# A two-layer spectral and gated-MLP mixer: one written-out order of named operations for a layer, and tables and weights loaded in halves

## The chip, the core and the metric

The kernel runs on one core of a Trainium2 chip. The core has a matrix engine (TensorE, PE in the profile; its weight loads are PEld), a vector engine (VectorE, DVE), a scalar engine (ScalarE, ACT), a general engine (GpSimd, POOL) and a queue engine for transfers (SyncE, SP). Each works through its own list of instructions in order, and semaphores make one wait for another. The metric is the device time of one execution in microseconds; lower is better. Before the change it is 402.71 us, the median of three runs.

## What is computed

The state `x` has 2048 rows of 512 values in bfloat16. Two layers follow each other, and each consists of block A and block B, with the same weights in both layers:

```
x = x + A(layernorm(x))
x = x + B(layernorm(x))

A(x):  X = rfft2(x) over rows and columns
       return irfft2(X * (w_r + i w_i))

B(x):  h  = gelu(layernorm(x) @ w1)                  # 512 x 512
       hs = four column groups of h, shifted by +1, -1, +2, -2 rows
       x1 = x + hs @ w2                              # 512 x 512
       h2 = gelu(layernorm(x1) @ w3) @ w4            # 512 x 1792, 1792 x 512
       return x1 + h2
```

## The kernel before, in words

The state lies in SBUF as `x_state`, 128 partitions by 16 slabs q by 512 columns; row 16 p + q of the input is partition p of slab q. The Fourier transform of block A is written as matrix products against small tables: over p (128 points), over the columns d, and over q (16 points), and back in the reverse order.

The stages, with the lines that the profile shows:

- `first_front` computes the statistics of the first layernorm for all 16 slabs, partly on DVE (`bn_stats`, L201) and partly on ACT (two passes with a running sum, L299 and L212), scales a table by the reciprocal deviation (`Tq`, L252), and does the transform over p (`over_p`, L263 and L265) into V. While ACT works through its passes, its queue also issues the loads of the tables TL (two halves) and TR.
- `middle` goes over 16 frequency blocks b, in units of one or two. `over_d` (L356) makes four matmuls of 256 columns for each b; ACT copies the result to TV. `over_q` (L369 to L371) makes two of 256 and one of 512; ACT copies to X. `weigh` multiplies X by the two planes of W on DVE (Pab, L382), then adds and subtracts the products into Z (L384, L385). `back_q` (L391, L392) makes four matmuls of 256 for each b, and the result is copied to M by ACT or, for the odd b up to 11 and half of b = 15, by DVE (L404). PSUM banks 0 and 1 belong to `over_d`, 2 and 3 to `over_q`, 4 to 7 to `back_q`. The order of these steps is written out in a string `ORDER`, with a name such as `d4` for `over_d` of the unit that begins at 4; each name stands for the matmuls and for the copies and products that follow them.
- `mlp` follows when all of M is there. `back_d` (L450) and `back_p` (L461) finish the inverse transform, a pair of slabs at a time, with ACT copying Y between them; DVE adds the result to the state (L467, L470), even slabs get `bn_stats` on DVE and odd ones a square on ACT. POOL computes from them the two reciprocal deviations that the nested layernorms need (`rstd_twice`, L236 to L242). Then, for four groups of four slabs: normalisation to `xn` (L245), transposes on PE (L493) copied by ACT to xT, `w1` (L508) with a gelu on ACT (L511) into hT, `w2` (L523) on the shifted hT with an add on DVE (L525), a square on ACT, normalisation to x1n, transposes again, and `w3` (L556), 14 blocks of 128 columns for each group with a gelu for each two blocks (L559) into gT, and `w4` (L565) with the add to the state on DVE (L567). The order of these steps is the order of the calls at the end of `mlp`. There all of the inverse transform comes first, `w1` and `w2` alternate with transposes, and the first blocks of `w3` stand among the last `w2`.
- At the end of the first layer, between the last `w4` steps, the next layernorm's statistics, the tables Tq and the transform over p of the second layer are computed; at the end of the second the result is stored.

In `mlp` all PSUM tiles are taken from one ring of eight banks (`banks`).

The schedule is manual: each engine executes its instructions in the order in which the Python code emits them. Loads are issued by SP (`x_state` in eight parts, then W, then G, Tinv, w1 to w4) and by ACT (T, FA, TL, TR). W is loaded plane by plane, w_r ahead of w_i, each with eight loads of 16 or 15 frequency blocks (L167 and L168, alternating) and one for the mirrored rows of b = 0 (L169).

## Time and profile before

| | |
|---|---|
| median of three runs | 402.71 us (402.16 to 403.85) |
| the profiled execution | 403.39 us |
| its span, first to last instruction | 401.4 us |
| PE busy (matmuls) | 359.1 us, 89% of the span |
| ACT busy | 218.8 us, 55% |
| DVE busy | 187.5 us, 47% |
| POOL busy | 63.0 us, 16% |
| mean granted clock of PE | 0.99 |
| moved by DMA | 15.16 MB |

A line of a group of instructions reads: line of the source, engine, operation, output <- inputs by their names in the program, shape, count | busy us, mean ns of one | idle time of the engine just before them, and what ended it. A line of the timeline begins with its start in us from the span's start and its duration; in square brackets stands the time that the engine sat idle before it, and what ended the wait. A line of the chain of work that ended last is start, duration and what ran. A line of the stretches reads: from and to, length, then for each engine the time busy and the number of instructions, then the clock granted to PE (1.00 is full), the share of the transfer engines that was busy, and GB/s. A line of a wait reads: who waited for whom, us in total, number of waits, the longest. Matmuls overlap in their pipeline, so the duration of one is longer than the distance from its start to the next one's.

### The profile page before, as it was taken

To read this page: it belongs to the slowest core of one execution; us is meant where nothing else is said; L and a number is where in the kernel's file an instruction comes from. 1 tells how busy PE (TensorE), PEld (TensorE's weight loads), DVE (VectorE), ACT (ScalarE), POOL (GpSimd) and SP (SyncE) were. 2 spreads that over 40 slices of the span, in tenths; PEclk is the share of its full clock that TensorE was granted. 3 is DMA by queue.
4 is the path that set the end of the run, shared out by engine and by line. 5 is a ranking of instruction groups with operands and counts; after the bars stand their busy time and mean duration, and the time that the engine had idled before them with its cause. 6 is when DMAs were issued, how large, how long until landed. Compare 5 with 4: busy or idle time off the path is not lost.

```text
span 401.4 us, 5501 instructions
## 1 busy us (share of the span) xinstructions
PE 359.1 (89%) x2109; PEld 199.5 (50%) x2144; DVE 187.5 (47%) x461; ACT 218.8 (55%) x327; POOL 63.0 (16%) x162
## 2 busy tenths in 40 slices
PE   0858978889999999999997887789999999999996
PEld 0635656645555444444555655665454544444442
DVE  4817849845346140411745786985445502020122
ACT  4756856887887405043034885788778731505200
POOL 3600004462130000010111000446213000000000
PEclk9998989999999999999999999999999999999999
DMA  8989300000000000000000000000000001010011
GB/s 268 343 184 355 121 0 0 2 2 0 2 1 2 0 0 2 0 0 2 0 2 1 0 2 0 2 1 2 1 2 0 2 13 41 0 39 15 15 51 41
DMA packets 12266, 15.16 MB, mean 38 GB/s; under 512 B 849, under 2 KB 10065, under 8 KB 12113
## 3 DMA queue, kind: packets, MB, share of 16 engines
q1 hardware_dynamic: 11520, 11.34, 9.2%
q10 hardware_dynamic: 720, 3.47, 2.5%
q8 instruction: 17, 0.28, 0.3%
q14 instruction: 9, 0.07, 0.0%
HBM read 12.71 MB, written 2.10 MB: 37 GB/s over the span
## 4 chain that ended last, share of the span: by engine, by line
PE 71%; DVE 10%; ACT 8%; DMA 6%; issue 3%; SPq 1%; ACTq 0%; DVEq 0%
PE ps L565 24%; PE ps L556 24%; PE ps L523 6%; PE ps L508 6%; DVE Pab L382 3%; PE ps L493 3%; DMA W<-in_A_w_r_dram 3%; PE ps L356 2%; ACT TV L142 2%; ACT xT L142 2%; DMA x_state<-in_A_x_dram 2%; PE ps L450 2%; ACT X L142 2%; DVE ln_st L201 1%; ACT Y L142 1%
## 5 line engine op out<-in xcount | busy, mean ns | idle before, releaser
L559 ACT ACTIVATE gT<-ps 128x1024 bf16<-128x1024 f32 x56 | 57.4, 1025 | 80.3 <-PE ps L556 54.4
L556 PE MATMUL ps<-xT,w 128*128 128x512 bf16 x436 | 98.5, 379 | 0.6
L565 PE MATMUL ps<-w,gT 128*128 128x512 bf16 x437 | 97.4, 379 | 0.6
L567 DVE TENSOR_TENSOR x_state<-ps,x_state 128x512 bf16<-128x512 f32 x32 | 22.1, 691 | 127.1 <-PE ps L565 104.3
L565 PEld LDWEIGHTS <-gT 128*128 128x128 bf16 x448 | 43.9, 98 | 52.4
L556 PEld LDWEIGHTS <-w 128*128 128x128 bf16 x448 | 43.6, 98 | 52.0
L525 DVE SCALAR_TENSOR_TENSOR xn<-xn,ln_c,ps 128x512 bf16<-128x512 bf16 x32 | 23.9, 748 | 27.3 <-PE ps L523 22.7
L508 PE MATMUL ps<-xT,w 128*128 128x512 bf16 x126 | 29.5, 379 | 3.9 <-ACT xT L142 3.8
L201 DVE BATCH_NORM_STATS2 ln_st<-x_state 128x6 f32<-128x512 bf16 x43 | 29.4, 683 | 5.8 <-DMA x_state<-in_A_x_dram 5.0
L142 ACT ACTIVATE xT<-ps 128x1024 bf16<-128x1024 bf16 x32 | 31.8, 1021 | 0.0
L382 DVE TENSOR_TENSOR Pab<-X,W 128x1024 bf16<-128x1024 bf16 (+1 forms) x40 | 21.6, 581 | 18.7 <-ACT X L142 10.0
L523 PE MATMUL ps<-w,hT 128*128 128x512 bf16 x124 | 29.9, 379 | 0.3
L217 POOL TENSOR_SCALAR ln_mv<-ln_s 128x4 f32<-128x4 f32 (+2 forms) x21 | 5.8, 275 | 145.9 <-ACT junk L212 145.4
L142 ACT ACTIVATE V<-ps 128x1024 bf16<-128x1024 f32 (+1 forms) x13 | 12.3, 972 | 28.7 <-PE ps L265 28.7
L263 PE MATMUL ps<-Tq,x_state 128*128 128x256 bf16 x64 | 16.3, 295 | 12.4 <-DVE Tq L252 12.3
L142 ACT ACTIVATE TV<-ps 128x1024 bf16<-128x1024 f32 (+1 forms) x20 | 21.5, 1087 | 9.5 <-PE ps L356 9.5
L212 ACT ACTIVATE junk<-xn 128x512 bf16<-128x512 bf16 x32 | 20.1, 630 | 10.0 <-DVE xn L525 8.5
L391 PE MATMUL ps<-TR,Z 128*128 128x256 bf16 x64 | 16.3, 279 | 9.0 <-DVE Z L384 9.0
L356 PE MATMUL ps<-FA,V 128*128 128x256 bf16 x128 | 17.8, 282 | 4.2 <-ACT TV L142 2.1
L508 PEld LDWEIGHTS <-w 128*128 128x128 bf16 x128 | 12.3, 98 | 17.2 <-issue 4.4
L461 PE MATMUL ps<-Y,Tinv 128*128 128x256 bf16 x128 | 16.3, 273 | 4.2 <-ACT Y L142 4.1
L226 POOL TENSOR_TENSOR ln_r<-ln_ve,mhalf 128x4 f32<-128x4 f32 (+1 forms) x19 | 17.8, 937 | 13.9 <-DVE ln_ve L225 12.7
(65 smaller groups left out, 433.4 us busy)
## 6 DMA issues: line engine op xcount, KB each, us to landing
w<-in_B_w_dram SPq DMA_DIRECT2D x2, 1792.0 KB, 12.6
x_state<-in_A_x_dram SPq DMA_DIRECT2D x8, 256.0 KB, 5.4
out_dram<-x_state SPq DMA_DIRECT2D x16, 128.0 KB, 1.8
TL<-tab_TL ACTq DMA_DIRECT2D x2, 768.0 KB, 7.6
TR<-tab_TR ACTq DMA_DIRECT2D x1, 1536.0 KB, 9.9
w<-in_B_w_dram SPq DMA_DIRECT2D x2, 512.0 KB, 4.9
W<-in_A_w_r_dram SPq DMA_DIRECT2D x4, 128.0 KB, 10.2
W<-in_A_w_i_dram SPq DMA_DIRECT2D x4, 128.0 KB, 4.5
```

What stands on the lines that cost most here:

```text
L142: K.nc.scalar.activation(dst, src, ACT.Copy, bias=0.0, scale=1.0)
L201: v.bn_stats(st[:], src)
L212: K.nc.scalar.activation(junk[:], src, ACT.Square, bias=0.0, scale=1.0, accum_out=self.s[:, i, 1:2])
L356: nc.tensor.matmul(ps[:, i, (1 - h) * 256:(2 - h) * 256], lhsT=V[:, 2 * t + h, b].rearrange("d q c -> d (q c)"), rhs=K.FA[:, t, h], start= ...
L382: nc.vector.tensor_tensor(t[pl][:, 0:n], X, w, op=ALU.mult)
L508: nc.tensor.matmul(ps[:, i], lhsT=K.w1[:, t, j * P:(j + 1) * P], rhs=xT[g][:, t, :], start=(t == 0), stop=(t == 3))
L523: nc.tensor.matmul(ps, lhsT=K.hT[:, j, st:st + P], rhs=K.w2[:, j, :], start=(j == 0), stop=(j == 3))
L525: nc.vector.scalar_tensor_tensor(xn[:, q, :], xn[:, q, :], L.c[:, q % 4:q % 4 + 1], ps, op0=ALU.mult, op1=ALU.add, accum_out=ln3[g].s[:, i ...
L556: nc.tensor.matmul(ps[:, t % 2], lhsT=K.w3[:, c, t * P:(t + 1) * P], rhs=xT3[g][:, c, :], start=(c == 0), stop=(c == 3))
L559: nc.scalar.activation(gT[g][:, t - 1:t + 1, :], ps, ACT.Gelu_apprx_tanh, bias=0.0, scale=1.0)
L565: nc.tensor.matmul(ps, lhsT=gT[g][:, t, i * P:(i + 1) * P], rhs=K.w4[:, t, :], start=(t == 0), stop=(t == 13))
L567: nc.vector.tensor_tensor(K.x[:, q, :], ps, K.x[:, q, :], op=ALU.add)
```

## The change

`middle` and `mlp` become one function, `layer`. Every step that used to be a function with matmuls and the copies behind them is cut into single operations with names of one letter, and a table maps the letter to the function: d, q, b, D, P, T, v, u, U, w are matmuls or transposes on PE; t, x, m, Y, e, h, k, F, g are copies, gelus and squares on ACT (m also on DVE); p, z, a, n, f, E, o work on DVE; s is a statistic on DVE for an even slab and a square on ACT for an odd one; r, c, R are small computations on POOL. A new string `ORDER` lists 341 names in the order in which they are emitted, from the first `over_d` of the layer up to the last of the `w3` blocks of groups 0 and 1. The loops for the `w3` blocks of groups 2 and 3, for `w4`, and for the next layer's front stay behind it as they were. What each operation computes, on which engine and in which shape, is unchanged, except for these points:

- `rstd_twice` is split: r (the deviation that the norm needs) stays, and the four operations for c, which `w2`'s add needs, form an operation of their own.
- The residual adds E, 16 in number, move from the middle of group 1's `w3` into the list.
- PSUM rings: d, q and b have their rings in the same banks as before, all else takes banks from the ring of eight.
- W is loaded in two halves over b (0 to 7, 8 to 15), both planes of the first half ahead of the second: 34 loads by SP instead of 18.
- TL and TR are loaded in two halves each, in the order TL, TR, TL, TR, issued by ACT's queue between the passes of `first_front`: four loads instead of three.
- The pool of small tiles has nine buffers instead of six.

The diff, cut to its core:

```diff
-    K.small = pool("small", 6)
+    K.small = pool("small", 9)
...
+RINGS = {"all": (0, 8), "d": (0, 2), "q": (2, 2), "b": (4, 4)}
...
-    for pl, w in enumerate((A_w_r, A_w_i)):
-        v = w.rearrange("(m j b) f -> m j b f", b=16, j=8)[:, :, :, 1:257]
-        for jj in range(4):
-            nc.sync.dma_start(K.W[jj * 2::8, pl], v[:, jj])
-            nc.sync.dma_start(K.W[jj * 2 + 1::8, pl, 1:16], v[:, 7 - jj, 15:0:-1])
-        nc.sync.dma_start(K.W[1::2, pl, 0], v[:, 4:8, 0])
-    K.load_TR = lambda: table("TR", nc.scalar)
+    for lo, hi in ((0, 8), (8, 16)):
+        for pl, w in enumerate((A_w_r, A_w_i)):
+            v = w.rearrange("(m j b) f -> j m b f", b=16, j=8)[:, :, :, 1:257]
+            b1 = max(lo, 1)
+            for jj in range(4):
+                nc.sync.dma_start(K.W[jj * 2::8, pl, lo:hi], v[jj][:, lo:hi])
+                nc.sync.dma_start(K.W[jj * 2 + 1::8, pl, b1:hi], v[7 - jj][:, 17 - hi:17 - b1][:, ::-1])
+            if lo == 0:
+                vm = w.rearrange("(m j b) f -> m j b f", b=16, j=8)[:, :, :, 1:257]
+                nc.sync.dma_start(K.W[1::2, pl, 0], vm[:, 4:8, 0])
...
+    loads = {5: ("TL", slice(0, 8)), 8: ("TR", slice(0, 8)), 11: ("TL", slice(8, 16)), 14: ("TR", slice(8, 16))}
...
-        if q in (5, 8):
-            K.load_TL(slice(0, 8) if q == 5 else slice(8, 16))
-    K.load_TR()
+        if q in loads:
+            K.load_q(*loads[q])
...
-    for op in ORDER.split():
-        b = int(op[1:])
-        if op[0] == "d":
-            over_d(units[b])
-        elif op[0] == "q":
-            over_q(units[b])
-        elif op[0] == "b":
-            got[b] = back_q(b)
-            take_M(*got[b], "S")
-        else:
-            take_M(*got[b], "V")
...
-ORDER = """d0 d1 q0 d2 q1 d4 q2 b0 b1 m1 d6 q4 b2 b3 m3 d8 q6 b4 b5 m5 d10 q8 b6 b7 m7 d12 q10 b8 b9 m9
-    d14 q12 b10 b11 m11 d15 q14 b12 q15 b13 b14 b15 m15"""
...
+    table = {"d": over_d, "t": take_d, "q": over_q, "x": take_q, "p": weigh, "z": weigh2, "b": back_q,
+             "D": back_d, "Y": take_D, "P": back_p, "a": add_x, "s": stats2, "r": rstd2, "c": lambda g: ln[g].ratio(), "n": norm2,
+             "T": tr, "e": take_T, "v": w1, "h": gelu1, "u": w2, "f": add_x1, "k": square3, "E": resid,
+             "R": rstd3, "o": norm3, "U": tr3, "F": take_U, "w": w3, "g": gelu3}
+    for op in ORDER.split():
+        if op[0] == "m":
+            take_b(int(op[1:-1]), op[-1])
+        else:
+            table[op[0]](int(op[1:]))
...
+ORDER = """
+d0 d1 t0 t1 q0 d2 t2 q1 d4 x1 p1 x0 q2 z1 t4 b1 p0 z0 x2 d6 m1V p2 q4 z2 t6 d8 x4 p4 q6 t8 b3 d10 z4 m3V x6 q8 t10
+b5 x8 d12 t12 p6 z6 m5V p8 q10 b6 b2 x10 d15 t15 z8 q12 p10 d14 m6A z10 x12 p12 b0 t14 m0A q15 z12 m2A b8 q14 m8A
+x15 b7 b4 m7V m4A b12 p15 b13 z15 b10 x14 m12A b9 p14 b15 m13A b11 m15A m15V z14 m9V m10A m11V b14 m14A D1 D0 Y1 Y0
+P2 a2 P3 D3 Y3 a3 P0 P1 D2 s2 a0 P6 s3 P7 a1 s0 Y2 a6 s1 D5 Y5 P5 D6 a7 P4 s6 r0 a5 a4 n1 D4 D7 n2 c0 P10 n3 Y6 s7
+s5 P11 P13 n0 s4 Y4 T0 a11 T1 a10 a13 r1 Y7 P9 a9 n5 e0 P14 P12 n6 e1 s9 s11 n4 n7 a14 P8 a12 s13 P15 v1 T2 e2 a8
+a15 T3 e3 s8 v0 v3 s10 h1 s14 c1 s12 v2 r2 h0 h3 s15 n11 r3 u0 n10 c3 n9 T5 h2 n8 c2 f0 T4 n13 e4 n12 u1 u3 u2 E0
+k0 n15 T6 n14 e5 f3 e6 f1 k3 f2 T7 v4 v5 k1 e7 v7 v6 h4 h5 u4 f4 u7 f7 u6 h7 k2 u15 R0 f6 o0 k4 u5 o1 E6 o3 f5 U0
+h6 o2 f15 u13 u9 f9 u12 F0 k7 E5 U1 k5 f13 k6 u14 k13 f12 u10 R1 k9 u8 E4 u11 F1 f10 f8 w0 k12 f14 E2 w3 f11 k15
+k10 o4 o6 E14 o5 k8 U2 k14 E11 g0 o7 R3 E10 U3 w4 F2 E13 w5 F3 o13 k11 E1 g3 o12 R2 g5 g4 w12 o14 w7 g12 E15 U6 o15
+F6 U7 w8 o9 g7 o8 w2 w9 F7 g8 g2 U4 w6 g9 F4 E12 g6 w13 g13 E8 o10 w11 o11 E9 g11 U5 w10 E7 w1 F5 g10 E3 g1
+"""
```

A number behind d, t, q, x, p or z is the unit by its first b; behind b and m the frequency block, with A or V for the engine of the copy; behind D and Y a pair of slabs; behind P, a, s and n a slab; behind u, f, k, E and o a row slab in the order 2, 3, ... 15, 0, 1; behind T, e, U and F a pair of slabs for the transposes; behind v and h a half group of w1; behind w and g a pair of w3 blocks (0 to 6 are group 0, 7 to 13 group 1).

More of the change, by code (lines that the diff above doesn't have):

```diff
@@ L127, with banks @@
     for last in (False, True):
-        middle(K)
-        mlp(K, last)
-def banks(K, n):
-    if K.ps_next + n > 8:
-        K.ps_next = 0
-    k = K.ps_next
-    K.ps_next = (k + n) % 8
-    return K.ps[:, k:k + n, :]
+        layer(K, last)
+RINGS = {"all": (0, 8), "d": (0, 2), "q": (2, 2), "b": (4, 4)}
+def banks(K, n, ring="all"):
+    lo, size = RINGS[ring]
+    k = K.ps_next.get(ring, 0)
+    if k + n > size:
+        k = 0
+    K.ps_next[ring] = (k + n) % size
+    return K.ps[:, lo + k:lo + k + n, :]
 def copy_act(K, dst, src):
@@ L338, in first_front, with layer @@
     take(3)
-def middle(K):
+def layer(K, last):
     nc = K.nc
@@ L455, in back_p @@
     def back_p(q):
[L456 to L463 removed]
+        ps["P", q] = o = banks(K, 1)[:, 0]
+        y = Y[q // 2][:, q % 2]
```

449 lines of the change are left out of this document (186 added, 263 removed).

## The prediction

> **What bounds the kernel now.** I read the page first, then the chain that ended last, the busy time by stretches, PE's waits, and last the order of events in the two places where PE waits longest.
>
> ```profile
> PE 359.1 (89%) x2109; PEld 199.5 (50%) x2144; DVE 187.5 (47%) x461; ACT 218.8 (55%) x327; POOL 63.0 (16%) x162
> PE 71%; DVE 10%; ACT 8%; DMA 6%; issue 3%; SPq 1%; ACTq 0%; DVEq 0%
> ```
>
> PE is the bound, but only 71% of the chain is PE; the rest is PE waiting for a copy, a product or a load. Where? I cut the span where PE starts the forward transform of a layer (first L356), the inverse one (L450) and the last multiplication (L565).
>
> ```profile
> core 0: us, PE busy (x) PEld busy (x) DVE busy (x) ACT busy (x) POOL busy (x), PEclk, DMA share, GB/s
> 21.96:55.53 33.57, 25.33 (x175) 17.10 (x178) 21.11 (x47) 23.59 (x30) 0.00 (x0) 0.95 0.60 186
> 55.53:135.76 80.23, 75.31 (x488) 43.80 (x496) 44.58 (x120) 61.38 (x102) 23.39 (x60) 0.98 0.00 1
> 217.57:246.83 29.26, 23.45 (x175) 16.55 (x177) 20.93 (x47) 23.11 (x30) 0.00 (x0) 1.00 0.00 1
> 246.83:325.14 78.31, 73.84 (x489) 42.99 (x497) 44.58 (x120) 60.13 (x101) 23.39 (x60) 1.00 0.00 1
> ```
>
> Call the first stretch of a layer A (d, q, b of the new table) and the second B (everything from D to the last w3 of the table). Rows one and two are layer 1, three and four layer 2. PE's busy time counts overlapping matmuls, so I set the work from PE's pace in the chain instead:
>
> ```profile
> 91.61 1.73 PE ps L508 x8
> 118.60 0.89 PE ps L493 x16
> 228.29 0.89 PE ps L356 x8
> ```
>
> That is 0.216 us for a matmul of 512 columns, 0.056 for a transpose, 0.111 for 256 columns. A has 160 of 256 (64 d, 32 q, 64 b) and 16 of 512: 17.8 + 3.5 = 21.3 us. B has 128 of 256 (D, P), 128 transposes and 240 of 512 (64 w1, 64 w2, 112 w3): 14.2 + 7.1 + 51.9 = 73.2 us. So PE idles, or runs slow, for 12.3 and 8.0 us in the two A, and 7.0 and 5.1 us in the two B: 32.4 us, all that reordering these stretches can give. What lies outside them (first front, last w3 and w4, second front) keeps its order of work.
>
> ```profile
> DVE Pab L382 <- DMA W<-in_A_w_i_dram: 8.5, 2, 5.0
> PE ps L391 <- DVE Z L384: 9.0, 14, 2.8
> PE ps L461 <- ACT Y L142: 4.1, 8, 1.0
> PE ps L508 <- ACT xT L142: 3.8, 4, 1.9
> ```
>
> PE's own waits in A are for Z, the weighted product; in layer 1 DVE in turn waits for the weights W. In B they are for copies by ACT.
>
> **Stretch A.** The edits move instructions and add none to PE, DVE or ACT here: the same 20 product pairs, the same copies. So which engine needs longest once nothing waits? By the rows above (layer 2), DVE has 20.9 us of work, ACT 23.1, PE 21.3. DVE cannot start at once, however. In the new order ACT does t0 t1 t2 x1 x0, so the first product p1 comes behind t2, which is behind d0 d1 q0 d2.
>
> ```profile
> 217.57 1.03 PE L356 MATMUL ps<-FA,V 128*128 128x256 bf16 x8 [0.93 <-DVE V L279]
> 220.50 1.32 ACT TV L142
> 52.12 0.59 ACT L142 ACTIVATE X<-ps 128x512 bf16<-128x512 f32 x1
> 52.61 0.60 ACT L142 ACTIVATE M<-ps 128x512 bf16<-128x512 f32 x1
> ```
>
> Before, t2 ended at 220.50 + 1.32 = 221.82, 4.25 us after the first matmul; PE's work ahead of it is the same now. One x copy more (0.49 us from its start to the next) gives 4.75. From there DVE's 20.9 us run to 25.65, if x comes in time for each product. ACT is through with its 23.1 us at about 24.5 (it starts 0.64 us in and waits some 0.75 us for d2), so it stays ahead of DVE, and PE's 21.3 us fit beside both. With 0.25 us to hand the last M over, **A takes 25.9 us**. Layer 2 gains 29.26 - 25.9 = **3.4 us**. Bounds: nothing, if ACT's and DVE's orders interlock no better than before; 4.5 us, if DVE is fed early enough that ACT's 24.5 us decide plus the same 0.25. I take the walk, which goes through the new order.
>
> Layer 1 would gain 33.57 - 25.9 = 7.7 us, if W came in time.
>
> ```profile
> TR<-tab_TR ACTq DMA_DIRECT2D x1, 1536.0 KB, 9.9
> 11.51 0.34 ACTq L152 DMA_DIRECT2D TR<-tab_TR  x1
> 6.18 0.68 SPq L167 DMA_DIRECT2D W<-in_A_w_r_dram  x1
> 17.08 1.00 SPq L169 DMA_DIRECT2D W<-in_A_w_r_dram  x1
> 21.45 0.55 SPq L168 DMA_DIRECT2D W<-in_A_w_i_dram  x1
> 25.96 0.60 SPq L169 DMA_DIRECT2D W<-in_A_w_i_dram  x1
> 24.73 0.42 DVE L382 TENSOR_TENSOR Pab<-X,W 128x512 bf16<-128x512 bf16 x1 [3.43 <-DMA W<-in_A_w_i_dram]
> 30.20 0.42 DVE L382 TENSOR_TENSOR Pab<-X,W 128x512 bf16<-128x512 bf16 x1 [5.04 <-DMA W<-in_A_w_i_dram]
> ```
>
> The tables TL and TR end at 11.51 + 9.9 = 21.4. Until then SP issued nine W loads (the whole of w_r) in 6.18 to 17.08, 1.36 us apart; from 21.45 to 25.96 eight came 0.64 us apart. DVE's first product could start at 24.73 (w_r there), its second at 30.20 (w_i there, 4.2 us after its last issue). The change issues 34 W loads instead of 18, of half the size, and the first 18 bring units b 0 to 7 of both planes: as many bytes as w_r. TL and TR keep their bytes and their place on ACT's queue, only cut and interleaved. So the first half cannot be there much before 24.7, when as many bytes were there before, and not after 30.2 unless halving costs pace; eighteen issues are more than nine, and at 0.64 us each a small load moves half the bytes of before. I take the middle, 27.5, an estimate. DVE asks at 21.96 + 4.75 = 26.7: 0.8 us late. **Layer 1's A gains 7.7 - 0.8 = 6.9 us** (bounds: 7.7 with W early; 4.2 with W at 30.2).
>
> The second half follows: last first-half issue at 27.5 - 4.2 = 23.3, sixteen more at 0.64 end at 33.6, landed 37.8. It is wanted by p8:
>
> ```profile
> 231.43 1.29 DVE L382 TENSOR_TENSOR Pab<-X,W 128x1024 bf16<-128x1024 bf16 x2 [0.93 <-ACT X L142]
> 233.44 0.68 DVE L404 CAST M<-ps 128x512 bf16<-128x512 f32 x1
> 234.04 1.29 DVE L382 TENSOR_TENSOR Pab<-X,W 128x1024 bf16<-128x1024 bf16 x2
> 242.85 0.75 DVE L382 TENSOR_TENSOR Pab<-X,W 128x512 bf16<-128x512 bf16 x2
> 244.05 0.76 DVE L382 TENSOR_TENSOR Pab<-X,W 128x512 bf16<-128x512 bf16 x2
> ```
>
> A pair of units costs DVE 2.01 us and its M copy 0.60, a single unit 1.20. Ahead of p8 stand two singles, three pairs and three M copies: 4.75 + 2.4 + 6.0 + 1.8 = 15.0 us after d0, so 36.9, with the 0.8 above 37.7. The second half is just in time: I price it at nothing, but nothing covers a later one. G, Tinv and w1 to w4 queue behind it on SP, some 8 us later than before; G is first used by D1 at about 48.7, so they cost nothing.
>
> The Trainium skill, "DMA: Bandwidth & Descriptors", section "Bandwidth", speaks against the cut: it asks for loads of 1 MiB, and measured 0.95 us for one of 64 KB (through another issuing engine). By that figure sixteen loads would take 15.2 us instead of 10.2, p8 would wait some 5 us, and the sum below would end near 392. The trace's 0.64 us for a load of twice the size decides for me; its descriptors were already rows of 512 bytes.
>
> **The clock.** PE lost time in layer 1 a second way.
>
> ```profile
> 28.00:31.00 3.00, 0.16 (x1) 0.00 (x1) 0.77 (x3) 0.96 (x2) 0.00 (x0) 1.00 0.55 168
> 33.00:35.00 2.00, 2.00 (x12) 1.41 (x10) 1.91 (x4) 0.02 (x1) 0.00 (x0) 0.50 1.02 369
> 55.50:58.90 3.40, 3.37 (x16) 2.41 (x17) 0.00 (x0) 1.02 (x1) 0.00 (x0) 0.50 0.00 0
> ```
>
> After 3 us with almost no matmul the granted clock fell to 0.50; it did so again at 55.5, where only short waits went before:
>
> ```profile
> 55.07 0.28 PE L450 MATMUL ps<-G,M 128*128 128x256 bf16 x1 [0.48 <-ACT M L142]
> ```
>
> The two stretches cost 1.0 and 1.7 us. My A has PE at work 21.3 of 25.9 us with no gap over 1 us, so I expect neither drop, and both are in the sums already. "TensorE: Matmul & The Clock Gate" in the Trainium skill, section "What's actually happening", lets the clock fall after an idle window of about 3.4 us; here it fell right after a wait of 0.48 us, so the measurement says that a drop can come with smaller gaps. I keep 1.7 us for one in the range.
>
> **Stretch B.** The work stays 73.2 us; what counts is the idle time left.
>
> ```profile
> L142 ACT ACTIVATE Y<-ps 128x1024 bf16<-128x1024 f32 x16 | 16.0, 1014 | 6.6 <-PE ps L450 6.6
> L559 ACT ACTIVATE gT<-ps 128x1024 bf16<-128x1024 f32 x56 | 57.4, 1025 | 80.3 <-PE ps L556 54.4
> L511 ACT ACT_TABLE_LOAD  x1: 1283/1283/1283, 76.2 to 76.2; - x1
> ```
>
> At its head D1 and D0 take 0.89 us each, and P2 needs Y1, copied in 1.01 from the end of D1: 0.2 us idle. From there each P stands two or more blocks behind its D, and transposes and w1 begin while P still runs, so the waits of 4.1 and 3.8 us have other matmuls under them. At the tail a new wait arises: w1 is the last pair of w3, its gelu g1 takes 1.03 us, and w4 needs it as its second pair; two of its matmuls (0.43) hide part: 0.6 us, where before group 1's w3 lay between. DVE's 16 adds, norms and statistics must keep up with P, and the ring of eight banks with the adds; for places that I cannot walk I leave a fifth of the 7.9 us that ACT's copies cost both layers, 1.6 us per layer, an estimate. Idle: 2.4 us. Layer 1 also has the one load of the gelu table, 1.2 us with PE waiting on the first gelus of w1. **B takes 76.8 and 75.6 us**: gains 80.23 - 76.8 = **3.4** and 78.31 - 75.6 = **2.7 us**. Bounds: none at all (a misplaced copy for each one saved), or 5.8 and 5.1 with no idle but the table's load.
>
> Splitting rstd_twice moves four of seven POOL operations behind the r that the norm waits for, but r was third already: nothing. The residual adds (E) move into B, on DVE with 44.6 us of 78 busy: nothing. One more DMA issue on ACT's queue costs its 0.34 us by the TR row at most; see also the third rival.
>
> **The sum.** 3.4 + 6.9 + 3.4 + 2.7 = 16.4 us. The profiled execution took 403.39 us (span 401.4), beside a median of 402.71 of three runs within 1.7 us. 403.39 - 16.4 = **387.0 us**.
>
> **Rivals.** *B gives nothing.* Every engine runs its list in order, so an operation placed too early holds all behind it; the table mixes a dozen kinds and leaves no slack. For: DVE's 44.6 and ACT's 60 us of work in B (rows above) must come between PE's blocks in just this order. Against: PE's old waits there were of one kind, a copy asked for at once. Only A gains, 10.3: 393.1 us.
>
> *W arrives too slowly: slower than before.*
>
> ```profile
> SPq L167 <- DMA TL<-tab_TL: 2.3, 1, 2.3
> 11.93 11.43 DMA W<-in_A_w_r_dram
> ```
>
> SP's loads wait for earlier loads to land, and one W load took 11.43 us under the tables' traffic. If it is the count of loads in flight and not their bytes that sets the pace, 34 loads go at the old 1.36 us: the last is issued at 6.18 + 33 x 1.36 = 51.1 and lands at 55.2; p8 waits 18.3 us instead of 0.8. 387.0 + 17.5 = 404.5, and two clock drops as above add 2.7: 407.2 us. It decides from a pace of about 1.25 us per load. Against it: 0.64 us once the tables are in.
>
> *ACT is held by its own load.* The fourth table load may wait for a W load's landing, as SP's did; then ACT's copies of V stand behind it. If it waits for the load above, landed at 23.4, all that stood behind the old TR issue (11.51) comes up to 11.9 us later, d0 at 33.9. W is then in time, D1 comes at 59.8 instead of 55.5: layer 1 loses 4.3 - 3.4 = 0.9, layer 2 keeps its 6.1. 398.2 us. Against: the fourth load takes the place in the queue where TR went out freely, ahead of that W load.
>
> *The order does not reach the engines*, and only the halves act: a small gain in layer 1, near 400.
>
> **How the numbers follow.** Forecast 0.70; B gives nothing 0.11; ACT held 0.08; W too slow 0.08; order without effect or losses that cancel 0.03. The range runs from 380.5 (W in time, A at 24.75, B nearly without idle) to 396 (B's rival, with a clock drop and W a microsecond later); outside it lie ACT held and W too slow, 0.16, and little else. 0.5%, 2.0 us, is about what a measurement of this kernel can tell: faster 0.89 (the first three), same 0.03, slower 0.08.
>
> **What would show it.** First d to first D1 in layer 2: 26 us, with DVE gapless from the first product on; 29 would refute A. Same stretch in layer 1: 26 to 27, DVE's wait for W under 1.5 us and none at p8; a granted clock of 1.0. D1 to first w4: 75 to 77 us, with a wait of w4 for gT of 0.6 us. Last W issue at about 33.6; later than 40 and W rules. ACT's first V copies a microsecond or so behind the last table issue. A time over 396 or under 380 means that a term above is missing.

## The result, and the profile after

The changed kernel takes **385.28 us** (385.09 to 386.24, four runs) beside 403.24 (402.16 to 403.85, four runs) of the kernel before on the same chip: a ratio of 0.956 with a 95% interval of 0.953 to 0.959, 18 us faster. The forecast was 387.0. The profiled execution took 385.34 us, its span is 383.4.

The page of the changed kernel, busy time by engine and the chain that ended last:

```profile
PE 354.7 (93%) x2144; PEld 198.7 (52%) x2144; DVE 184.6 (48%) x461; ACT 214.7 (56%) x327; POOL 67.2 (18%) x162
PE 80%; ACT 8%; DMA 6%; DVE 3%; issue 1%; SPq 1%; POOL 1%; ACTq 0%; DVEq 0%; POOLq 0%
```

The counts of instructions on DVE, ACT and POOL are those of before, so no engine has less to do. What changed is the chain: PE is 80% of it instead of 71%, DVE 3% instead of 10%. The stretches begin at the first d, the first D and the first w4 of each layer; the columns are those of the stretches in the prediction:

```profile
21.58:49.02 27.44, 22.96 (x177) 16.91 (x177) 20.72 (x47) 22.68 (x30) 0.00 (x0) 1.00 0.67 204
49.02:123.48 74.46, 73.76 (x496) 42.95 (x497) 43.44 (x120) 60.28 (x102) 25.48 (x60) 1.00 0.04 14
123.48:206.15 82.67, 80.01 (x401) 39.04 (x400) 30.88 (x71) 21.67 (x22) 6.14 (x10) 1.00 0.00 1
206.15:233.02 26.87, 22.84 (x177) 16.97 (x177) 20.72 (x47) 22.70 (x30) 0.00 (x0) 1.00 0.00 1
233.02:306.35 73.33, 73.09 (x497) 43.13 (x498) 43.44 (x120) 58.71 (x101) 25.48 (x60) 1.00 0.00 1
306.35:383.40 77.05, 72.85 (x337) 32.71 (x335) 11.07 (x16) 15.36 (x15) 0.00 (x0) 0.99 0.08 28
```

Beside the rows of before, with each stretch's saving (measured: difference of the two profiled executions):

| stretch | before | after | saved | forecast |
|---|---|---|---|---|
| start to d0, layer 1 | 21.96 | 21.58 | 0.38 | 0 |
| A, layer 1 | 33.57 | 27.44 | 6.13 | 6.9 |
| B, layer 1 | 80.23 | 74.46 | 5.77 | 3.4, the new wait of w4 included |
| first w4 to d0 of layer 2 | 81.81 | 82.67 | -0.86 | 0 |
| A, layer 2 | 29.26 | 26.87 | 2.39 | 3.4 |
| B, layer 2 | 78.31 | 73.33 | 4.98 | 2.7, the new wait of w4 included |
| first w4 to the end | 76.26 | 77.05 | -0.79 | 0 |
| sum | 401.4 | 383.4 | 18.0 | 16.4 |

(81.81 is 217.57 - 135.76 and 76.26 is 401.4 - 325.14, from the rows of before.) One boundary is not quite the same: the rows of before begin B at 55.53 and 246.83, where the second D matmul starts, while the first starts 0.46 us earlier, at 55.07 and 246.37. With the first D matmul as the boundary in both kernels, A saves 5.67 and 1.93 us and B 6.23 and 5.44; the sum stays.

Stretch B of layer 2 is now 73.33 us long and PE is busy for 73.09 of them: nothing is left there to reorder. In layer 1 PE's timeline shows two short waits in B, of which layer 2 has only the first, and one behind B, which the prediction had priced at the tail:

```profile
51.16 1.03 PE L446 MATMUL ps<-Y,Tinv 128*128 128x256 bf16 x8 [0.24 <-ACT Y L145]
78.01 0.62 PE L480 MATMUL ps<-ident,xn 128*128 128x128 bf16 x8 [0.36 <-DVE xn L256]
...
123.48 0.59 PE L579 MATMUL ps<-w,gT 128*128 128x512 bf16 x2
124.76 1.47 PE L579 MATMUL ps<-w,gT 128*128 128x512 bf16 x6 [0.68 <-ACT gT L562]
```

After two w4 matmuls PE stands 0.68 us until g1, the last gelu, has written gT. The boundary puts this wait behind the first w4, outside B; it is why the stretches from w4 on are 0.86 and 0.79 us longer.

In stretch A the first D waits for DVE's last M copy, but DVE is not gapless before it. DVE's timeline in A of layer 2 (first d at 206.15):

```profile
210.86 0.76 DVE L403 TENSOR_TENSOR Pab<-X,W 128x512 bf16<-128x512 bf16 x2 [4.76 <-ACT X L145]
...
216.23 1.29 DVE L403 TENSOR_TENSOR Pab<-X,W 128x1024 bf16<-128x1024 bf16 x2 [0.29 <-ACT X L145]
...
230.85 0.42 DVE L425 CAST M<-ps 128x256 bf16<-128x256 f32 x1 [0.54 <-ACT M L145]
...
231.59 1.28 DVE L425 CAST M<-ps 128x512 bf16<-128x512 f32 x2
```

The first product comes 4.71 us after d0. From it to the end of the last M copy (231.59 + 1.28 = 232.87) are 22.01 us, 1.1 more than DVE's work of 20.9: 0.29 waiting for x4, 0.54 for ACT's half of the M copy of b = 15, the rest in gaps too small to be printed. ACT's last M copy (b = 14, 232.27 to 232.87) ends at the same time; the matmuls that it copies had waited for z14 on DVE, which stands behind the wait of 0.54 us.

And W in layer 1, DVE's first products and p8, and SP's issues:

```profile
26.30 0.42 DVE L403 TENSOR_TENSOR Pab<-X,W 128x512 bf16<-128x512 bf16 x1 [5.38 <-DMA W<-in_A_w_i_dram]
27.60 0.42 DVE L403 TENSOR_TENSOR Pab<-X,W 128x512 bf16<-128x512 bf16 x1 [0.88 <-DMA W<-in_A_w_i_dram]
...
37.47 1.28 DVE L403 TENSOR_TENSOR Pab<-X,W 128x1024 bf16<-128x1024 bf16 x2
```

```profile
21.80 0.55 SPq L173 DMA_DIRECT2D W<-in_A_w_i_dram  x1
...
35.14 0.60 SPq L174 DMA_DIRECT2D W<-in_A_w_i_dram  x1
```

The second product, which needs the imaginary plane, starts at 27.60; p8 at 37.47 has no wait. The wait of 0.88 us belongs to this execution: in five other profiled executions with the same loads (runs below) the two products run as one, from 24.51 at the earliest. The granted clock is 1.00 in both A and both B.

### The profile page after: what moved, and what is told of

Its sections match the earlier page's. It is cut to its first block, busy times and chain, and to the rows that moved or that the text cites. A ratio compares the mean times of both kernels' runs of the same rounds, so it can differ in the third digit from the quotient of the medians.

```text
span 383.4 us, 5555 instructions
## 1 busy us (share of the span) xinstructions
PE 354.7 (93%) x2144; PEld 198.7 (52%) x2144; DVE 184.6 (48%) x461; ACT 214.7 (56%) x327; POOL 67.2 (18%) x162
## 4 chain that ended last, share of the span: by engine, by line
PE 80%; ACT 8%; DMA 6%; DVE 3%; issue 1%; SPq 1%; POOL 1%; ACTq 0%; DVEq 0%; POOLq 0%
PE ps L555 25%; PE ps L579 25%; PE ps L518 6%; PE ps L502 6%; PE ps L446 4%; ACT TV L145 3%; PE ps L480 3%; PE ps L434 3%; PE ps L372 3%; DMA W<-in_A_w_r_dram 2%; DMA TL<-tab_TL 2%; DMA x_state<-in_A_x_dram 1%; PE ps L416 1%; ACT X L145 1%; PE ps L417 1%
## 5 line engine op out<-in xcount | busy, mean ns | idle before, releaser
L224 POOL TENSOR_SCALAR ln_mv<-ln_s 128x4 f32<-128x4 f32 (+2 forms) x21 | 6.6, 313 | 116.2 <-ACT junk L219 115.6
L372 PE MATMUL ps<-FA,V 128*128 128x256 bf16 x128 | 16.9, 272 | 5.6 <-ACT TV L145 3.0
L518 PEld LDWEIGHTS <-hT 128*128 128x128 bf16 x128 | 12.3, 98 | 14.2 <-ACT hT L509 0.8
L145 ACT ACTIVATE Y<-ps 128x1024 bf16<-128x1024 f32 x16 | 15.9, 1021 | 5.8 <-PE ps L434 3.0
```

What stands on the lines that cost most here:

```text
L145: K.nc.scalar.activation(dst, src, ACT.Copy, bias=0.0, scale=1.0)
L372: nc.tensor.matmul(o[:, i, (1 - h) * 256:(2 - h) * 256], rhs=K.FA[:, t, h], lhsT=V[:, 2 * t + h, b].rearrange("d q c -> d (q c)"), start=( ...
L518: nc.tensor.matmul(o, lhsT=K.hT[:, j, st:st + P], rhs=K.w2[:, j, :], start=(j == 0), stop=(j == 3))
```

## The experiments

The theory to be tested: the gains of A and B are separate and add; in A, DVE's first product plus DVE's work sets the end; the halves of W matter for layer 1 alone. The rivals are named with each run. In the first four, one part of the change is undone or done alone. Each ratio is to the kernel before, run beside it (medians there from 402.42 to 403.47 us). Times of two variants are compared by their medians, which may come from different chips, so differences under a microsecond say little by themselves.

### The new order with the old loads

```diff
-    for lo, hi in ((0, 8), (8, 16)):
-        for pl, w in enumerate((A_w_r, A_w_i)):
...
+    for pl, w in enumerate((A_w_r, A_w_i)):
+        for jj in range(4):
+            nc.sync.dma_start(K.W[jj * 2::8, pl], v[:, jj])
...
-    loads = {5: ("TL", slice(0, 8)), 8: ("TR", slice(0, 8)), 11: ("TL", slice(8, 16)), 14: ("TR", slice(8, 16))}
+    loads = {5: ("TL", slice(0, 8)), 8: ("TL", slice(8, 16)), 14: ("TR", slice(0, 16))}
```

> The new order with the loads as they were before (W plane by plane in 18 loads, TL in halves, then TR whole). My theory, that the order gives nearly all: only layer 1's forward stretch changes; W's second plane is there at about 30.2 us instead of 27.6, so d0 to D1 in layer 1 grows by 2.6 us, and by 1 to 2 more if the clock drops behind the wait; 388 to 390 us. Rival, that the early W is what makes the order work: the list is in order and p1 holds up everything, so more than 5 us are lost, 391 us or more. Other rival, that the halves matter for nothing: 385 to 386 us.

Measured: 389.54 us (389.17 to 389.61), ratio 0.968 (0.963 to 0.973). Only A of layer 1 is longer. Its row, and DVE's second product:

```profile
21.81:53.17 31.36, 24.62 (x177) 17.65 (x177) 20.74 (x47) 22.98 (x30) 0.00 (x0) 0.95 0.68 200
```

```profile
30.27 0.43 DVE L399 TENSOR_TENSOR Pab<-X,W 128x512 bf16<-128x512 bf16 x1 [3.31 <-DMA G<-tab_G]
```

31.36 instead of 27.44 us, with a clock of 0.95. The second product starts at 30.27, as it did before the change (30.20). The view names G, but a product does not read G: it is what landed last by the records; what DVE needs is W. The halves, of W and of the tables together, are worth 4.3 us.

### The old order with the new loads

The load loops and the dictionary of table loads of the changed kernel, put into the kernel before.

> The old order with tables and W loaded in halves. My theory: DVE's second product in layer 1 starts at about 27.6 us instead of 30.2, the rest of layer 1 moves up by 2.6 us, and if the half-clock stretch at 33 us goes too by 1 us more; layer 2 unchanged: 399.5 to 401 us. Rival, halves matter for nothing: 403 us. Rival, W's second half comes too late for a faster consumer: a new wait for W at the unit of b = 8, and 402 us or more.

Measured: 398.85 us (398.17 to 399.43), ratio 0.991 (0.987 to 0.994).

```profile
22.43:51.38 28.95, 24.05 (x177) 16.30 (x177) 20.80 (x47) 23.23 (x30) 0.00 (x0) 1.00 0.69 209
```

A of layer 1 falls from 33.11 (55.07 - 21.96, cut at the first D matmul alike) to 28.95, since the earlier W also takes away the stretch at half clock (1.00 instead of 0.95). Layer 2 does not change. 398.85 is a little under what was expected. The halves are worth 4.4 us with the old order and 4.3 with the new.

### The new order in A alone, and in B alone

`ORDER` is mixed: the new string up to the last m and the old sequence of `mlp` behind it, or the old sequence of `middle` and the new string from D1 on. The new loads are in both.

> The changed kernel, with the names from D1 on put back into the sequence that the old calls gave; the forward part and the loads stay new. If the gains of the two stretches add: layer 2's second stretch goes from 73.3 back to about 78.3 us less the tail wait of 0.7 that the old sequence doesn't have; layer 1's likewise by 4 to 5 us; 394 to 395 us. Rival, that the second stretch only gained because the first one ended in a better state (clock, banks): under 390 us.

Measured: 393.45 us (392.96 to 393.81), ratio 0.978 (0.974 to 0.982).

```profile
21.62:48.48 26.86, 22.86 (x176) 17.00 (x177) 20.77 (x47) 22.68 (x30) 0.00 (x0) 1.00 0.68 211
48.48:127.60 79.12, 74.32 (x497) 43.06 (x498) 44.58 (x120) 61.22 (x102) 23.30 (x60) 1.00 0.03 11
```

> The changed kernel, with the names up to the last b and m put back into the sequence of the old string; the rest and the loads stay new. If the gains add: 2.4 us are lost in layer 2 and about 3.5 in layer 1 (6.1 less the 2.6 that the loads gave): 390 to 392 us, up to 393.5 if the clock drops again in layer 1. Rival, that the forward order gains nothing by itself: 386 us.

Measured: 390.88 us (389.47 to 391.68), ratio 0.971 (0.967 to 0.976).

```profile
21.83:50.63 28.80, 23.49 (x177) 16.44 (x177) 20.62 (x47) 23.11 (x30) 0.00 (x0) 1.00 0.71 218
50.63:125.44 74.81, 73.94 (x496) 42.96 (x497) 43.85 (x121) 60.25 (x102) 25.75 (x60) 1.00 0.01 3
```

From the kernel with the new loads alone (398.85), A's order gives 5.4 us and B's 8.0, together 13.4; both together gave 398.85 - 385.28 = 13.6. The gains add. (393.45 is half a microsecond under what was expected.) With the 4.4 of the loads A is worth 9.8 us, for which the prediction had 10.3, and B 8.0, for which it had 6.1. The table above gives A less and B more, 8.5 and 10.75 (9.1 with the new wait of w4), because it goes by place: B of layer 1 is 79.12 us with the old B behind the new A, but 80.69 in the kernel before (from the first D matmul alike). So some 1.6 us of the time saved in B of layer 1 were the stretch at half clock at its head, which went with the new loads and the new A. What B's 8.0 are made of, the order, the places of c and of the adds E, was not taken apart.

### The tail and the last product

w1 and g1 change places with w8 and g8, so that group 0's last gelu comes earlier; and DVE's half of the M copy of b = 15, which waited 0.54 us for ACT's half, moves behind two operations.

```diff
- ... F6 U7 w8 o9 g7 o8 w2 w9 F7 g8 g2 ... U5 w10 E7 w1 F5 g10 E3 g1
+ ... F6 U7 w1 o9 g7 o8 w2 w9 F7 g1 g2 ... U5 w10 E7 w8 F5 g10 E3 g8
...
- b11 m15A m15V z14 m9V m10A
+ b11 m15A z14 m9V m15V m10A
```

> Two exchanges in the changed kernel's list. In the w3 part the names w1 g1 and w8 g8 change places, so that the last pair of w3 belongs to group 1 and not to the group that w4 takes first. In the forward part z14 and m9V go ahead of m15V, which waits for ACT's copy of the other half of b = 15. If the two waits seen in the changed kernel are real and nothing is late behind them: PE's wait for gT of 0.68 us ahead of the third w4 matmul vanishes in both layers, and d0 to D1 in layer 2 falls by about 0.5 us from 26.87: 2.4 us less in all, 383 us. Rival, that D1 waits for the last M copies on DVE, whatever their order: only 1.4 us less, 384 us. Rival, that both are covered by something else: 385.3.

Measured: 382.95 us (382.29 to 383.25), ratio 0.952 (0.949 to 0.954). PE at the first w4:

```profile
122.22 1.24 PE L555 MATMUL ps<-xT,w 128*128 128x512 bf16 x5
123.30 2.97 PE L579 MATMUL ps<-w,gT 128*128 128x512 bf16 x13
```

The 13 matmuls run without the wait behind the second; from w4 to d0 it is 81.81 us again, as before the change, and A of layer 2 is 26.47 instead of 26.87. So the new wait cost 0.86 a layer in all, and it was avoidable.

### The second halves of the tables on SP's queue

The loads of the second halves of TL and TR leave ACT's queue and go out on SP, TL's behind the first half of W and TR's behind the second.

```diff
     for lo, hi in ((0, 8), (8, 16)):
         ...
+        k = ("TL", "TR")[lo // 8]
+        nc.sync.dma_start(getattr(K, k)[:, 8:16], dram[k][:, 8:16])
...
+    loads = {5: ("TL", slice(0, 8)), 8: ("TR", slice(0, 8))}
```

> The second halves of TL and TR go to SP's queue: TL's behind the first half of W, TR's behind the second; ACT issues only the first halves. Theory, that the tables' traffic starves W and that W then goes by 0.64 us a load: 1.5 MB less in front of W end the tables some 4 us earlier, the first half of W lands by 25.5 and DVE's first products in layer 1 start at about 26.3 for x1 instead of ending a wait at 27.6; d0 to D1 in layer 1 falls by 0.6 to 1.3 us, to 384 to 384.7 us. Rival, that the count of SP's loads alone sets the time of W: two more loads are in front, no gain or 0.6 us more. Rival, that the late tables come too late for q8 or b8: PE waits for TL or TR there, more than 386 us.

Measured: 384.52 us (384.38 to 385.69), ratio 0.956 (0.953 to 0.959): 0.8 us by the medians, which the intervals do not tell from nothing. In its profile A of layer 1 is 26.87 us instead of 27.44, and the first two products run as one from 26.00, without the second wait:

```profile
26.00 0.80 DVE L405 TENSOR_TENSOR Pab<-X,W 128x512 bf16<-128x512 bf16 x2 [5.38 <-DMA W<-in_A_w_r_dram]
```

That is not shown to be the tables' doing. With the tables loaded as in the changed kernel, A of layer 1 is 26.86 us in the profile of the new A with the old B, also without the second wait: the landing of W differs from execution to execution. What the move does take away is a wait of ACT. In the kernel with the tail's exchange, which loads as the changed kernel does, ACT's last table load went out only at 15.16, its copies of V stood behind it, and PE waited for them:

```profile
15.54 4.69 ACT L145 ACTIVATE V<-ps 128x1024 bf16<-128x1024 f32 x5 [2.97 <-DMA W<-in_A_w_r_dram]
```

```profile
16.61 0.27 PE L274 MATMUL ps<-Tq,x_state 128*128 128x256 bf16 x1 [1.55 <-ACT V L145]
```

d0 came at 22.34 there and at 22.52 in one more execution with these loads (ACT's wait 3.05 us), at 21.58 in the changed kernel's profile, and at 21.28 to 21.38 in the three profiles with the tables on SP's queue.

### W in quarters

```diff
-    for lo, hi in ((0, 8), (8, 16)):
+    for lo, hi in ((0, 4), (4, 8), (8, 12), (12, 16)):
```

> W in four quarters instead of two halves: 66 loads by SP instead of 34, the same bytes, everything else as in the changed kernel. If the number of loads sets the pace (0.64 us for each issue, whatever its size, the prediction's rival on W): the last W issue comes near 55 instead of 35.1, the product p12 (41.76 in the changed kernel) starts near 57, the first D of layer 1 near 64.7 instead of 49.0, and the time is 401 to 405. If the bytes set the pace, an issue of half the size takes half as long, the last issue stays near 35, and the time is 385 to 387.

Measured: 398.31 us (one run). The rows of SP's last W issue, of DVE where it waits for the last quarter, and of ACT's first copies of V:

```profile
50.36 0.59 SPq L174 DMA_DIRECT2D W<-in_A_w_i_dram  x1
```

```profile
47.48 0.69 DVE L403 TENSOR_TENSOR Pab<-X,W 128x1024 bf16<-128x1024 bf16 x1 [1.27 <-DMA W<-in_A_w_r_dram]
52.58 0.69 DVE L403 TENSOR_TENSOR Pab<-X,W 128x1024 bf16<-128x1024 bf16 x1 [4.40 <-DMA W<-in_A_w_i_dram]
```

```profile
18.76 0.33 ACTq L166 DMA_DIRECT2D TR<-tab_TR  x1
19.13 3.77 ACT L145 ACTIVATE V<-ps 128x1024 bf16<-128x1024 f32 x4 [3.56 <-DMA W<-in_A_w_i_dram]
```

The same bytes in twice as many loads cost 13 us, of which 1.2 are a stretch at half clock in layer 2 (A there is 28.06 us); A of layer 1 ran at a mean clock of 0.90, which is in the rest. Once the tables are in, the count sets the pace and not the bytes, 0.64 us an issue for halves and quarters alike; before that, the smaller loads went out closer to each other (the first 14 issues of halves from 5.80 to 21.80, 1.23 us apart, the first 18 of quarters from 5.49 to 18.98, 0.79 apart). It came out 3 us better than the lower end expected, because the last issue is at 50.4 and not at 55, and one part was not expected at all: ACT's last table load waits for a W load of SP's to land, and V's copies stand behind it. d0 starts at 26.71 instead of 21.58, 5.1 of the 13 us. So two rivals of the prediction, W too slow and ACT held by its own load, come true at once; in the profile of the changed kernel the same wait of ACT is 1.34 us long, and d0 comes no later than before the change (21.58, 21.96); in the two executions of the section above it was about 3 us long and d0 came 0.8 and 0.9 us later:

```profile
14.44 4.69 ACT L145 ACTIVATE V<-ps 128x1024 bf16<-128x1024 f32 x5 [1.34 <-DMA W<-in_A_w_r_dram]
```

### What holds A: DVE's work or ACT's copies

A took 26.87 us where 25.9 were forecast. The next two runs ask why. The first takes two M copies from DVE and gives them to ACT (1.2 us less work for DVE, by its row of 0.60 each). The second brings the first product forward.

```diff
- ... d10 z4 m3V x6 ... p6 z6 m5V p8 ...
+ ... d10 z4 m3A x6 ... p6 z6 m5A p8 ...
```

> Two of DVE's M copies (b = 3 and 5) go to ACT, at the same places of the list. By the theory of the prediction, that DVE's work decides the forward stretch, d0 to D1 in layer 2 falls from 26.87 by up to 1.2 us, to 25.7. Rival, that the alternation of d and t over the same two PSUM banks decides (PE 1.05 us, ACT 1.33 us, in turn): every ACT copy put between two t delays the next t, and the stretch grows by 0.3 to 1.0 us.

Measured: 389.05 us (one run). DVE's waits in layer 2:

```profile
218.99 1.29 DVE L403 TENSOR_TENSOR Pab<-X,W 128x1024 bf16<-128x1024 bf16 x2 [0.28 <-ACT X L145]
222.06 1.29 DVE L403 TENSOR_TENSOR Pab<-X,W 128x1024 bf16<-128x1024 bf16 x2 [0.98 <-ACT X L145]
...
227.16 1.29 DVE L403 TENSOR_TENSOR Pab<-X,W 128x1024 bf16<-128x1024 bf16 x2 [0.83 <-ACT X L145]
```

From p4 (218.99) to the first D (236.61) are 17.62 us, where the changed kernel has 233.02 - 216.23 = 16.79. DVE has less to do and ends later: it waits for X, which ACT copies. (Some 1.2 us of the 389.05 are a stretch at half clock ahead of p4, and belong to neither theory.) Layer 1, at full clock and with W in time, agrees: A is 27.72 us, 0.85 more than the 26.87 that the changed kernel's list takes where W is in time.

```diff
- d0 d1 t0 t1 q0 d2 t2 q1 d4 x1 p1 x0 q2 z1 t4 b1 p0 z0 x2 d6
+ d0 d1 t0 t1 q0 d2 x0 p0 z0 t2 q1 d4 x1 p1 q2 z1 t4 b1 x2 d6
```

> x0 p0 z0 go ahead of t2, so DVE's first product starts about 2 us earlier, in the gap in which ACT waits for d2. By the prediction's walk (DVE's first product plus 20.9 us of DVE work decide) 1.2 us of DVE work leave the front of the queue, and d0 to D1 in layer 2 falls from 26.87 to about 25.7. Rival, the alternation of d and t: x2 and x4 come no earlier, DVE waits for them longer, and the stretch stays at 26.6 to 26.9. In layer 1 W comes too late for either to show.

Measured: 386.26 us (one run). In layer 2:

```profile
208.91 0.76 DVE L403 TENSOR_TENSOR Pab<-X,W 128x512 bf16<-128x512 bf16 x2 [3.15 <-ACT X L145]
211.77 0.76 DVE L403 TENSOR_TENSOR Pab<-X,W 128x512 bf16<-128x512 bf16 x2 [1.57 <-ACT X L145]
...
217.13 1.29 DVE L403 TENSOR_TENSOR Pab<-X,W 128x1024 bf16<-128x1024 bf16 x2 [0.34 <-ACT X L145]
```

The first product comes 3.10 us after d0 (205.81) instead of 4.71, and DVE gives it back in waits for X (1.2 us of these are again a stretch at half clock). From p4 to D are 16.78 us, as in the changed kernel. Layer 1 shows it without a drop of the clock, since W was there in time after all:

```profile
24.51 0.95 DVE L403 TENSOR_TENSOR Pab<-X,W 128x512 bf16<-128x512 bf16 x2 [3.36 <-ACT X L145]
```

The first product comes 2.70 us after d0 (21.81), and A takes 26.88 us, as it does without the exchange where W is in time (26.86 and 26.87). So what decides up to p4 is when ACT delivers x, not when DVE begins. Two causes were left: d and t alternate over two PSUM banks, since one unit of d fills both (2.44 us a unit in the changed kernel), or ACT's own work, 1.32 for t and 1.02 for x.

### Four banks for d

```diff
-RINGS = {"all": (0, 8), "d": (0, 2), "q": (2, 2), "b": (4, 4)}
+RINGS = {"all": (0, 8), "d": (0, 4), "q": (4, 2), "b": (6, 2), "B": (0, 4)}
...
-    K.ps_next = {}
+    K.ps_next = {"all": 4}
...
-        ps["b", b] = banks(K, 1, "b")[:, 0]
+        ps["b", b] = banks(K, 1, "b" if b in (0, 1, 2, 3, 5, 6) else "B")[:, 0]
```

> The order is that of the changed kernel; only PSUM is dealt out anew in stretch A: the d steps take four banks instead of two, the back_q steps two (and, from the tenth on, the four of d), q stays at two. Theory now held: x4, which p4 waits for at 216.23 in layer 2 of the changed kernel, comes at the pace of the alternation d, t over two banks (2.44 us for a pair, PE's 1.05 and ACT's 1.33 one behind the other). With four banks d runs ahead of t, p4 starts 1.0 to 1.5 us earlier, and A in layer 2 falls from 26.87 to between 25.4 and 26.0; in layer 1 the wait for W remains, 27.44 becomes 26.5 to 27.4; time 383 to 384.5. Rival: DVE's first product and its work set A, as the prediction had it: A stays at 26.9 and the time at 385. Second rival: b needs four banks more than d does; A grows.

Measured: 383.51 us (383.07 to 384.65), ratio 0.951 (0.948 to 0.955). ACT's copies in A of layer 2 of the changed kernel, and then with four banks:

```profile
209.08 1.30 ACT L145 ACTIVATE TV<-ps 128x1024 bf16<-128x1024 f32 x1 [0.96 <-PE ps L372]
...
211.57 1.32 ACT L145 ACTIVATE TV<-ps 128x1024 bf16<-128x1024 f32 x1 [0.25 <-PE ps L372]
...
214.01 1.32 ACT L145 ACTIVATE TV<-ps 128x1024 bf16<-128x1024 f32 x1 [0.25 <-PE ps L372]
```

```profile
210.06 1.34 ACT L145 ACTIVATE TV<-ps 128x1024 bf16<-128x1024 f32 x1
...
212.61 1.32 ACT L145 ACTIVATE TV<-ps 128x1024 bf16<-128x1024 f32 x1 [0.24 <-PE ps L372]
...
214.69 1.33 ACT L145 ACTIVATE TV<-ps 128x1024 bf16<-128x1024 f32 x1
```

With two banks every t waits 0.25 us for PE and a unit takes 2.44; with four every second one does and two units take 4.63, 2.32 each, about what t and x need of ACT itself. DVE's wait ahead of p4 is gone. But A of layer 2 is 26.60, not 25.4 to 26.0, and 0.37 of what is missing is only that d0 now starts earlier against its copies (t0 is 1.00 us behind it instead of 0.64). So the banks were the smaller part, and the time inside 383 to 384.5 came in part by another way: of A of layer 1, 26.26 instead of 27.44, a good part is W, which this execution had in time at 26.47, and the stretch from w4 to d0 of layer 2 is 82.21 instead of 82.67.

### All of it together, and t2 on DVE

The tail, the late tables and the four banks in one kernel:

> All that gained together: w1 and g1 earlier in the tail, m15V behind z14 exchanged, the second halves of TL and TR behind the first half of W on SP's queue, and four banks for d. If the gains add: 1.4 to 2 us from the tail and z14, 0.6 from the tables, 1 to 2 from the banks: 381 to 382.5. If d's two banks were not what held x4: 382.3 to 383, as without them.

Measured: 381.69 us (380.63 to 382.12), ratio 0.946 (0.942 to 0.950), inside the bounds. But the gains overlap: by the medians the three kernels gained 2.3, 0.8 and 1.8 us each, 4.9 in all, and together 3.6. Its A of layer 1, and DVE's first product there:

```profile
21.28:47.31 26.03, 22.36 (x176) 17.03 (x177) 20.66 (x47) 22.73 (x30) 0.00 (x0) 1.00 0.79 248
```

```profile
26.02 0.80 DVE L405 TENSOR_TENSOR Pab<-X,W 128x512 bf16<-128x512 bf16 x2 [5.40 <-ACT X L145]
```

W is in time, and the first product waits for ACT alone. From it to D are 21.3 us.

Then the copy t2 goes to DVE, which is idle there, so that ACT has 1.3 us less ahead of x1, x0 and t4:

```diff
+        if u == 2:
+            for i in range(n):
+                nc.vector.tensor_copy(dst[:, i], src[:, i])
+        else:
+            copy_act(K, dst, src)
```

> All the gains together as before, and besides the copy t2 (TV of the third unit) on DVE, which stands idle for 5 us there, in place of ACT: two copies of 512 columns, 1.28 us by the row of two M copies. ACT loses 1.3 us of work ahead of x1, x0 and t4. Theory now held: with four banks for d, A is DVE's first product plus DVE's work (26.02 and 21.3 us in layer 1 of the kernel with all the gains), and the first product hangs on ACT's row t0 t1 t2 x1 x0. Then the first product comes 0.5 to 0.7 us earlier (DVE ends t2 some 4.1 us after the first d) and, as ACT is ahead as well, A falls from 26.0 to 25.4 in both layers: 380.3 to 380.8 us. Rival: ACT's alternation of t and x (2.2 us a pair) holds p4 and p6 as soon as the first product is earlier, as with x0 pulled ahead: DVE waits for X there and A stays at 26.0, 381.7 us. Second rival: t4 and d6 stand behind the copy on DVE and A grows.

Measured: **379.25 us** (379.14 to 379.33), ratio 0.939 (0.937 to 0.942), a microsecond better than expected; why better is partly a stretch at half clock that it no longer has (last section). DVE in A of layer 2 (first d at 202.36):

```profile
205.21 1.35 DVE L385 CAST TV<-ps 128x512 bf16<-128x512 f32 x2 [2.45 <-PE ps L374]
206.71 0.76 DVE L410 TENSOR_TENSOR Pab<-X,W 128x512 bf16<-128x512 bf16 x2 [0.15 <-ACT X L145]
...
226.02 1.61 DVE L432 CAST M<-ps 128x512 bf16<-128x512 f32 x3
```

```profile
202.36:227.87 25.51, 22.38 (x174) 17.06 (x177) 22.29 (x50) 21.46 (x29) 0.00 (x0) 1.00 0.00 1
```

The first product comes 4.35 us after d0, and from it to the end of the last M copy are 227.63 - 206.71 = 20.92 us without a printed wait; D follows 0.24 later. That is the sum which the prediction had made for A, term by term, once ACT is in time. A of layer 1 is 25.16. This is the fastest version, 24 us under the kernel before and 6 under the change.

## Why the prediction was right, and where its terms were off

It was right within 1.7 us in the profiled execution (387.0 against 385.34), by luck in part: A was forecast too short by 1.8 us and B too long by 3.3, and the two errors partly cancel.

**What bounds the kernel.** Right: PE does the same work and the gain is PE's idle time in A and B. In before the two stretches held 32.4 us of it; the change took 19.3, the four savings of A and B in the table.

**A: too good by 0.8 and 1.0 us.** The first product was right to 0.04 us (4.71 for 4.75). The step that failed is "ACT is through with its 23.1 us at about 24.5 [...], so it stays ahead of DVE". A total says that ACT ends early, not that it delivers each x in time. With less work for DVE, and with an earlier first product, A did not get shorter; with work taken from ACT it did, and DVE ran its 20.9 us through. The missing 1.1 us were DVE's gaps: x4, M of b = 15, and small ones; putting z14 ahead of m15V alone took 0.40 us off A (26.47). Of the forecast gains, 0.46 us in each layer were B's and not A's, since the old A was counted up to the second D matmul.

**The halves of W: right, the time of the first half by luck.** It was forecast for 27.5, the middle between two bounds, and the second product ran at 27.60, after a wait of 0.88 us for the 0.8 forecast. But with the same loads both planes were there for the first two products at 26.34 to 27.24 in four other profiled executions, and at 24.51 in a fifth; A of layer 1 was then 26.86 to 26.88 where the order was the change's or x0's exchange. So the term is 0.6 us (27.44 less 26.87) in one execution and nothing in others. p8 was forecast at 37.7 with the second half just in time; it ran at 37.47 without waiting. SP's pace was 0.64 us and the last issue 35.14 for 33.6. The Trainium skill, "DMA: Bandwidth & Descriptors", section "Bandwidth", has a rule that speaks against small loads. Its price, by which p8 would have waited 5 us in the prediction's estimate, did not show. The quarters agree with the rule's direction: twice the number of loads cost some 12 us.

**B: too cautious by 1.7 and 1.6 us.** With the 0.68 us of the tail counted in, as the prediction did, B took 75.14 and 74.01 us for 76.8 and 75.6. The forecast head (0.2; 0.24 measured), tail (0.6; 0.68) and table load (1.2; the two B differ by 1.13, the wait of 0.36 us in layer 1 included) are all there. What is not there is the allowance of 1.6 us per layer "for places that I cannot walk". The 7.9 us behind it are rows, 4.1 and 3.8; the fifth of them is not. It was also taken twice: the 7.9 us are the waits of both layers together, so a fifth is 0.8 us a layer. With 0.8 the sum would have been 385.4, and its closeness luck, since A's error would have covered what was still too much in B. This order has no such places: the 0.36 us are the one wait printed in 148 us besides the two walked. At what price a less careful order would have them was not tried.

**The clock.** No drop in the profiled execution of the changed kernel, as forecast. The reason given, no gap over 1 us in A, does not decide it: several variants had one in layer 2 after the same waits (last section), and of the changed kernel's own four executions one (386.24 us) has a mean clock of 0.995 beside 0.999 in the others.

**The rivals.** B gives nothing: refuted by the new B alone, which is worth 8.0 us. The order does not reach the engines: refuted. W too slow, and ACT held by its own load: both mechanisms are real, as the quarters show, and the changed kernel lies on the safe side of the first. The second costs it up to 1.2 us, depending on the execution (d0 at 21.58 to 22.52 with its loads, at 21.28 with the tables on SP's queue). The prediction's argument against ACT held, that the fourth table load takes a place in the queue ahead of the slow W load, does not hold in general: with quarters it went out only at 18.76, and V's copies waited 3.56 us behind it; with the halves it went out at 14.06 in one profile and at 15.16 in another.

## What to carry to other kernels

In a schedule written by hand, walk the supplier of each wait, not only its total: an engine with enough time over the stretch can still be late for each single step in its first third, and moving one copy to an engine that is idle just then was worth 1.3 to 2.4 us where an earlier first product alone had brought nothing. One profiled execution is not a term: where a load lands can differ by some 3 us in the next one. An allowance without a row is worth as much as a guess in either direction. When loads are cut so that the first part comes earlier, count the issues: halving paid 4.3 us here, quartering lost some 12.

## What was not expected of the hardware

**Loads of one queue hold computing on another engine.** ACT's own load waited for SP's W loads to land, with ACT's copies behind it (3.56 us with quarters, 1.34 and up to 3.05 with halves). What releases a wait is inferred from semaphore events, so whether the chip or the program's use of semaphores links the two queues is open; it was not tried.

**The half clock comes and goes.** Of six executions of the kernel with all gains but t2 three had a mean clock of 0.996 and took 381.97 to 382.12 us, three had 1.000 and took 380.63 to 381.41: one and the same list of instructions. In six of the ten profiled variants with the change's A, or nearly, the stretch lies at the start of layer 2's A; it makes this 28.05 to 28.07 us instead of 26.87 where the order there is the change's, which is the 1.2 us named above. The row of the kernel with m3 and m5 on ACT, which had it:

```profile
208.00:211.00 3.00, 3.00 (x15) 1.87 (x14) 0.00 (x0) 1.49 (x2) 0.00 (x0) 0.53 0.00 0
```

PE's longest waits ahead of it were 1.33 and 0.93 us; with the tables on SP's queue waits of 1.05 and 0.93 us at the same place brought a drop, and in the profiled execution of the changed kernel waits of 1.05 and 0.93 us brought none. In the Trainium skill, "TensorE: Matmul & The Clock Gate", section "What's actually happening", the window of about 3.4 us runs on its own, whatever the kernel does, and the clock falls after a whole idle window. The first fits that the drop depends on the execution; the second does not fit these two waits. In the version with t2 on DVE the five times lie within 0.2 us of each other, at a clock of 0.999 or 1.000; what keeps the drop away there was not tried. Against the three undisturbed executions without t2 on DVE, at least 1.3 us of the gain is not the clock's (380.63 less 379.33).
